# A decode attention kernel: the softmax bias moved from GpSimd to ScalarE, and the pipeline around it respaced

## Chip, cores and metric

The kernel runs on one core of a Trainium2 chip. The metric is device time in microseconds (us), the median over executions. A profile gives the span from the first to the last instruction, about 2 us less than the device time (819.8 against 821.6 us). A run counts as slow when it is over 1.5% above the fastest of the same kernel; fast runs are compared with fast runs.

Engines are named as in the profile: PE is TensorE (PEld is its loading of weights), DVE is VectorE, ACT is ScalarE, POOL is GpSimd, SP is the engine that issues the DMAs. "POOLq" or "SPq" is the sequencer of an engine.

## The reference

There are two grouped-query attention blocks for one new token, with separate inputs. Each has a batch of 4, 32 query heads, 8 key/value heads and a head size of 128. Problem A attends to all 4096 cached keys; problem B only to the last 1024.

```python
q = (x @ wq).reshape(B, 1, 32, 128)                  # x: 4 x 1 x 512, wq: 512 x 4096
scores = einsum("bhqd,bhkd->bhqk", q, k) * 128**-0.5 # k, v repeated 4x over heads
p = softmax(scores)
o = einsum("bhqk,bhkd->bhqd", p, v)
out = o.reshape(B, 1, 4096) @ wo                     # wo: 4096 x 512
# result: concatenate(A's out, B's out)
```

Almost all of the work is reading: the caches and weights are 100.7 MB in bf16, and each byte is used for a few products only.

## The kernel before

The work is cut into 40 units of 1 MB of K and 1 MB of V: 32 of problem A (one batch, one key/value head, 4096 keys) and then 8 of problem B (four batches, one head, 1024 keys each). For one unit:

1. SP loads K and V into SBUF, the working memory. PE transposes K in 32 blocks of 128x128 into PSUM, the memory for PE's results, in four groups of eight; DVE copies each group to SBUF.
2. PE computes the scores (32 matmuls of 4 columns). DVE reduces them to a maximum per partition. POOL makes the maximum over all partitions (a partition all-reduce), and multiplies it by minus the scale: that is the bias.
3. ACT computes the exponentials with that bias. DVE sums them per partition, and POOL sums over partitions with a second all-reduce (the denominator).
4. PE multiplies by V, DVE normalises, and for every group of heads PE adds the output projection.

POOL's loop and ACT's wait are what the argument is about:

```python
for t in range(self.NU):                       # 40 units
    self.wait(g_, f"dve.red.{t}")
    g_.partition_all_reduce(self.bm[:, s, 0:w], self.pm[:, s, 0:w], 128, ReduceOp.max)
    self.wait(g_, f"pool.max.{t}")
    ...
    g_.tensor_scalar(out=self.biasT[:, s, 0:w], in0=self.bm[:, s, 0:w],
                     scalar1=-self.scale, scalar2=None, op0=ALU.mult)
    if t - self.Ld >= 0:
        self._pool_den(g_, t - self.Ld)        # waits dve.rsum, partition_all_reduce(add)

# ACT, per unit
    self.wait(act, f"pool.bias.{i}")
    self.wait(act, f"pe.s.{i}")
    ...   # 4 exponentials of 128x32 (A) or 16 of 128x8 (B), bias=biasT column

# DVE, per step t
    self._dve_kcopies(dve, t + 2)
    self._dve_reduce(dve, t)
    self._dve_rowsum(dve, t - 1)
    self._dve_norm(dve, t - 1)                 # waits pool.den.{t-1}

# PE, per step t
    self._pe_transposes(pe, t + 1)             # two PSUM banks for the groups
    self._pe_scores(pe, t)
    self._pe_pv(pe, t - 2)
    # the output projection of unit t - 4; the whole second q projection after step 26
```

In DVE's program the copies for the next unit stand behind the wait for the denominator. In the trace DVE waits 20.53 us for POOL's denominator, starts the reciprocal at 306.20 us and the next copies at 306.49 us. A result that is late on POOL therefore holds up these copies, and through them PE and the freeing of load buffers.

## Time and profile before

| | before |
|---|---|
| device time, median of 5 | 824.1 us (819.7 to 825.1) |
| span of the profiled run | 819.8 us |
| busy: PE, DVE, ACT, POOL | 30%, 17%, 6%, 5% |
| mean DMA rate | 124 GB/s |
| mean granted PE clock | 0.527 |

The page of the kernel before: its busy line, and rows of 40 equal slices of the span (PEclk in tenths of full clock, DMA in tenths of busy, GB/s moved).

```profile
PE 244.2 (30%) x4168; PEld 210.3 (26%) x4168; DVE 136.4 (17%) x325; ACT 50.3 (6%) x257; POOL 44.7 (5%) x128
...
PEclk9855555555555555555555555565555555555555
DMA  8993222222223272222222333323833333110000
GB/s 355 388 405 135 103 102 103 104 103 103 103 103 103 103 307 103 103 103 103 103 103 103 107 106 124 118 86 109 277 103 108 124 123 109 52 52 1 1 1 1
```

No engine is busy, PE's granted clock is about half from the third slice on, and after three slices the loads fall from about 400 to about 103 GB/s. Nothing in this view is at a limit, so the kernel is held by waiting, not by work.

The waits, longest in total (engine, line, waited for: us in total, times, longest us):

```profile
ACT e_sb L350 <- POOL biasT L266: 733.9, 40, 23.6
DVE rden L639 <- POOL den L290: 621.1, 40, 21.3
...
POOL biasT L266 <- issue: 342.4, 40, 12.3
POOL den L290 <- issue: 244.3, 39, 10.9
```

ACT waits 734 of 820 us for the bias and DVE 621 us for the denominator; both come from POOL. POOL itself has 342 + 244 us before its own instructions in which it waits for nothing that the profile shows ("issue").

The timeline of POOL alone in steady state (start us, duration us, engine, line, operation, and in brackets the idle time before it and what ended it):

```profile
305.72 0.44 POOL L290 PARTITION_ALL_REDUCE den<-acc  x1 [10.88 <-issue]
310.14 0.38 POOL L254 PARTITION_ALL_REDUCE bm<-pm  x1 [3.98 <-DVE pm L608]
319.05 0.26 POOL L266 TENSOR_SCALAR biasT<-bm 128x4 f32<-128x4 f32 x1 [8.53 <-issue]
325.30 0.44 POOL L290 PARTITION_ALL_REDUCE den<-acc  x1 [5.99 <-issue]
```

One unit takes 19.6 us, from 305.72 to 325.30. The recorded work is 1.1 us. Between the all-reduce for the maximum and the multiply lie 8.5 us, and between the multiply and the next all-reduce 6.0 us. The wait of 3.98 us for DVE is the only one with a visible cause. The unit is typical, but for the 10.88 us before its first line: in the whole trace 36 of the 39 unexplained waits before the denominator's all-reduce are 5.8 to 6.3 us (the others 7.0, 8.8 and 10.9), and 38 of the 40 before the multiply are 6.9 to 9.2 us (the others 10.3 and 12.3).

Is an all-reduce itself slow, and its record only too short? At the end of the program two all-reduces follow each other. The timeline of all engines there:

```profile
812.77 0.44 POOL L290 PARTITION_ALL_REDUCE den<-acc  x1 [5.98 <-issue]
...
813.62 0.28 DVE L624 TENSOR_REDUCE acc<-e_sb 128x16 f32<-128x128 bf16 x1
...
814.00 0.44 POOL L290 PARTITION_ALL_REDUCE den<-acc  x1 [0.79 <-DVE acc L624]
...
814.48 0.25 DVE L639 RECIPROCAL rden<-den 128x16 f32<-128x16 f32 x1 [0.58 <-POOL den L290]
```

The second all-reduce starts 0.1 us after DVE's sum ends (813.62 + 0.28), and DVE goes on at 814.48. So an all-reduce after an all-reduce costs about half a microsecond; the 6 us are not its own.

### The profile page before, as it was taken

The numbers are of one execution on the slowest core, as the hardware profiler recorded it, in microseconds if no ns is written. First come the engines' busy times: TensorE is split into PE (matmuls) and PEld (weight loads), VectorE is DVE, ScalarE is ACT, GpSimd is POOL, SyncE is SP. The second block draws the span as 40 slices with busy tenths as digits, with TensorE's granted clock in tenths as the row PEclk, the third lists the DMA queues.
The fourth block names the chain that finished last, engine by engine and source line by source line (L and its number), as shares of the span: only waits on it lengthen the run. The fifth ranks groups of instructions, "written<-read, shape, count | busy, mean of one in ns | idle before, by whom it ended". The sixth has DMA issues, their size and how long they took to land.

```text
span 819.8 us, 9559 instructions
## 1 busy us (share of the span) xinstructions
PE 244.2 (30%) x4168; PEld 210.3 (26%) x4168; DVE 136.4 (17%) x325; ACT 50.3 (6%) x257; POOL 44.7 (5%) x128
## 2 busy tenths in 40 slices
PE   3512222322232303232323332332222322333323
PEld 3412222222222203232312232322222322222211
DVE  1401111111111101121111111121111111111100
ACT  0000000000000000000000000000000001111211
POOL 0000000000000000000000000000000000000000
PEclk9855555555555555555555555565555555555555
DMA  8993222222223272222222333323833333110000
GB/s 355 388 405 135 103 102 103 104 103 103 103 103 103 103 307 103 103 103 103 103 103 103 107 106 124 118 86 109 277 103 108 124 123 109 52 52 1 1 1 1
DMA packets 27019, 101.31 MB, mean 124 GB/s; under 512 B 1360, under 2 KB 9568, under 8 KB 17760
## 3 DMA queue, kind: packets, MB, share of 16 engines
q1 hardware_dynamic: 26976, 100.69, 33.4%
q8 instruction: 33, 0.54, 0.3%
q14 instruction: 10, 0.08, 0.0%
HBM read 100.67 MB, written 0.01 MB: 123 GB/s over the span
## 4 chain that ended last, share of the span: by engine, by line
issue 89%; POOL 5%; PE 2%; DMA 2%; DVE 1%; POOLq 1%; ACT 0%; SPq 0%
POOL den L290 2%; POOL bm L254 2%; DMA big_w<-in_A_wq_dram 2%; PE KTps L442 1%; POOL biasT L266 1%; DVE KT L592 1%; PE outp L512 0%; PE psT L416 0%; POOLq L266 0%; POOLq L290 0%; PE psT L471 0%; ACT e_sb L350 0%; DVE out_sb L572 0%; DVE rden L639 0%; DVE pm L608 0%
## 5 line engine op out<-in xcount | busy, mean ns | idle before, releaser
L442 PE MATMUL KTps<-ident,rawKd 128*128 128x128 bf16 x896 | 101.6, 304 | 334.2 <-DVE KT L592 334.2
L442 PEld LDWEIGHTS KTps<-ident,rawKd 128*128 128x128 bf16 x896 | 87.3, 141 | 349.0 <-DVE KT L592 341.4
L592 DVE COPY KT<-KTps 128x1024 bf16<-128x1024 bf16 x160 | 106.5, 687 | 28.5 <-PE KTps L442 28.0
L639 DVE RECIPROCAL rden<-den 128x4 f32<-128x4 f32 (+1 forms) x40 | 7.7, 193 | 621.1 <-POOL den L290 621.1
L442 PE MATMUL KTps<-ident,big_w 128*128 128x128 bf16 x384 | 44.2, 307 | 181.2 <-DVE KT L592 168.3
L350 ACT ACTIVATE e_sb<-psT,biasT 128x32 bf16<-128x32 f32 (+1 forms) x256 | 49.0, 330 | 733.9 <-POOL biasT L266 733.9
L442 PEld LDWEIGHTS KTps<-ident,big_w 128*128 128x128 bf16 x384 | 38.1, 143 | 185.7 <-DVE KT L592 171.3
L491 PE MATMUL oT<-e_sb,V 128*128 128x4 bf16 x1280 | 39.7, 166 | 42.5 <-ACT e_sb L350 42.5
L491 PEld LDWEIGHTS oT<-e_sb,V 128*128 128x128 bf16 x1280 | 37.2, 104 | 44.5 <-issue 44.5
L471 PEld LDWEIGHTS psT<-qT_sb,KT 128*128 128x128 bf16 x1280 | 41.6, 106 | 0.9 <-issue 0.9
L471 PE MATMUL psT<-qT_sb,KT 128*128 128x4 bf16 x1280 | 41.1, 167 | 0.0
L290 POOL PARTITION_ALL_REDUCE den<-acc x40 | 17.7, 443 | 245.1 <-issue 244.3
L266 POOL TENSOR_SCALAR biasT<-bm 128x4 f32<-128x4 f32 (+1 forms) x40 | 10.6, 264 | 342.4 <-issue 342.4
L254 POOL PARTITION_ALL_REDUCE bm<-pm x40 | 15.5, 387 | 172.5 <-DVE pm L608 165.8
L512 PE MATMUL outp<-big_w,OT_all 128*4 128x512 bf16 x32 | 14.8, 621 | 1.4 <-DVE OT_all L646 1.4
L512 PE MATMUL outp<-wo_sb,OT_all 128*4 128x512 bf16 x32 | 14.1, 590 | 0.0
L624 DVE TENSOR_REDUCE acc<-e_sb 128x4 f32<-128x128 bf16 (+1 forms) x40 | 11.1, 277 | 10.8 <-ACT e_sb L350 10.8
L608 DVE TENSOR_REDUCE pm<-psT 128x4 f32<-128x128 f32 (+1 forms) x40 | 11.2, 281 | 0.0
L646 DVE TENSOR_TENSOR OT_all<-oT,rden 128x4 bf16<-128x4 f32 (+1 forms) x40 | 6.9, 173 | 1.4
L512 PEld LDWEIGHTS outp<-big_w,OT_all 128*4 128x4 bf16 x32 | 2.9, 107 | 7.8 <-issue 5.1
L416 PE MATMUL psT<-xT_sb,big_w 128*128 128x4 bf16 x128 | 3.6, 166 | 3.5 <-DMA big_w<-in_A_wq_dram 3.5
L416 PEld LDWEIGHTS psT<-xT_sb,big_w 128*128 128x128 bf16 x128 | 3.5, 104 | 3.6 <-DMA big_w<-in_A_wq_dram 3.6
(18 smaller groups left out, 15.7 us busy)
## 6 DMA issues: line engine op xcount, KB each, us to landing
V<-in_A_v_cache_dram SPq DMA_DIRECT2D x32, 1024.0 KB, 5.1
rawKd<-in_A_k_cache_dram SPq DMA_DIRECT2D x22, 1024.0 KB, 7.4
big_w<-in_A_k_cache_dram SPq DMA_DIRECT2D x10, 1024.0 KB, 7.3
V<-in_B_v_cache_dram SPq DMA_DIRECT2D x8, 1024.0 KB, 5.6
rawKd<-in_B_k_cache_dram SPq DMA_DIRECT2D x6, 1024.0 KB, 8.2
big_w<-in_A_wq_dram SPq DMA_DIRECT2D x1, 4096.0 KB, 12.6
wo_sb<-in_A_wo_dram SPq DMA_DIRECT2D x1, 4096.0 KB, 29.0
big_w<-in_B_wq_dram SPq DMA_DIRECT2D x1, 4096.0 KB, 14.8
```

Of the source, the lines that this page charges most:

```text
L254: g_.partition_all_reduce(self.bm[:, s, 0:w], self.pm[:, s, 0:w], 128, bass.bass_isa.ReduceOp.max)
L266: g_.tensor_scalar(out=self.biasT[:, s, 0:w], in0=self.bm[:, s, 0:w], scalar1=-self.scale, scalar2=None, op0=ALU.mult,)
L290: g_.partition_all_reduce(self.den[:, s, 0:w], self.acc[:, s, 0:w], 128, bass.bass_isa.ReduceOp.add)
L350: ins = act.activation(self.e_sb[:, se, b * C:(b + 1) * C, h], ps[:, b * C:(b + 1) * C, h], ACT_F.Exp, bias=self.biasT[:, sy, idx:idx + 1] ...
L442: ins = pe.transpose(self.KTps[kb][:, k, :], self.Rq(r)[:, q0 + k, :], self.ident128[:, :],)
L471: ins = pe.matmul(ps[:, q, :], lhsT=KTv[:, q, :], rhs=qT, start=True, stop=True)
L491: ins = pe.matmul(self.oT[ob][:, b * 4:(b + 1) * 4], lhsT=self.Vq(s)[:, q, :], rhs=self.e_sb[:, se, q, :], start=(c == 0), stop=(c == C - 1),)
L512: ins = pe.matmul(self.outp[0:self.NB, :], lhsT=self.OT_all[P][:, h, :], rhs=self.wo_sb[P][:, h, :], start=(h == 0), stop=(h == self.HQ - 1),)
L592: ins = dve.tensor_copy(dst[:, q0:q0 + ng, :], self.KTps[kb][:, 0:ng, :])
L608: ins = dve.reduce_max(self.pm[:, sy, 0:w], ps, axis=AX.X)
L624: ins = dve.reduce_sum(self.acc[:, sy, 0:w], ev, axis=AX.X)
L639: ins = dve.reciprocal(self.rden[:, sy, 0:w], self.den[:, sy, 0:w])
```

## The change

The intent was to take the multiply off POOL and then let the rest of the pipeline run closer. The diff has about 300 lines; this is its core.

```diff
 # POOL: only all-reduces are left in the loop
             self.inc(ins, "pool", f"pool.max.{t}")
-            self.wait(g_, f"pool.max.{t}")
-            if t - NY >= 0:
-                self.wait(g_, f"act.exp.{t - NY}.last")
-            ins = g_.tensor_scalar(out=self.biasT[:, s, 0:w], in0=self.bm[:, s, 0:w],
-                                   scalar1=-self.scale, scalar2=None, op0=ALU.mult)
-            self.inc(ins, "pool", f"pool.bias.{t}")
 # ACT: the bias is a copy with a scale
-        self.wait(act, f"pool.bias.{i}")
+        self.wait(act, f"pool.max.{i}")
+        ins = act.activation(self.biasT[:, sy, 0:w], self.bm[:, sy, 0:w], ACT_F.Copy,
+                             scale=-self.scale)
+        self.inc(ins, "act", f"act.bias.{i}")
+        self.wait(act, f"act.bias.{i}")
 # configuration: lead of the copies, banks for transposes, lead of the K loads
-    LK=2,
+    LK=1,
+    NKTB=4,
-    KLEAD=2,
+    KLEAD=3,
 # PE: values before scores, second q projection in eight chunks instead of at once
             if t + LT < self.NU:
                 self._pe_transposes(pe, t + LT)
+            if 0 <= i < self.NU:
+                k = step - self.QB0
+                if 0 <= k < self.NPIECE:
+                    self._pe_qTB_chunk(pe, i, k)
+                self._pe_pv(pe, i)
             if t < self.NU:
                 self._pe_scores(pe, t)
-            if 0 <= i < self.NU:
-                self._pe_pv(pe, i)
...
 # SP: four K and four V blocks asked for in advance, weights in pieces
+        for t in range(NRD):
+            self._issue_k(sp, t)
+        for t in range(NRD):
+            self._issue_v(sp, t)
...
+            for P, key in ((0, "wo0_at"), (1, "wo1_at")):
+                p = t - self.cfg[key]
+                if 0 <= p < self.NPIECE:
+                    self._issue_wo(sp, P, p)
```

To get the two further PSUM banks for transposes, the result of the value product moved into a free part of the score bank. A switch for filler matmuls and one for loads that transpose are in the diff but turned off.

## The prediction

> **What bounds the kernel now.** The page's busy table shows no full engine: PE 30%, DVE 17%, ACT 6%, POOL 5%, and DMA moves 101.3 MB at a mean of 124 GB/s. The chain of waits is 89% "issue", through POOL's three lines. In the time-ordered listing one unit of steady state (POOL operations at 305.72, 310.14, 319.05, 325.30 us) is 19.6 us: an all-reduce for the maximum (0.38 us), 8.5 us in which POOL shows nothing, the small multiply for the bias (0.26 us), 6.0 us of nothing, the all-reduce for the denominator (0.44 us), then 4.0 us in which POOL waits for DVE. 40 units of 19.6 us are 784 of the 820 us. The waits agree: ACT waits 734 us for the bias, DVE 621 us for the denominator.

> The two gaps are not the all-reduce itself. Where one all-reduce follows another, there is no gap: at the end (812.77, then 814.00 us) the second starts 0.1 us after DVE's sum ends, and DVE goes on 0.6 us after that sum. So a gap comes with each change between the all-reduce and the ordinary multiply. [...]the trace has 5.9 to 6.2 us into the all-reduce, and 7 to 8.8 us the other way.

> **What the change does.** The multiply goes to ACT as a copy with a scale; POOL then runs only all-reduces in the loop. That removes about 14.5 us from every unit's chain and adds some 0.3 us on ACT. [...]I expect still one table load (1.28 us now). The rest (four transpose banks, loads issued earlier and in pieces, second projection in eight chunks) serves a pipeline that isn't POOL-bound.

> **The new bound.** Estimates per unit of problem A from the trace's durations: DVE four copies 2.7, two reductions and the wait for POOL about 1.3, normalising 0.3: 4.3 us. PE 4.2 us at full clock (transposes 66 ns, as at 24 to 31 us) but 6.3 us at half clock (118 ns). POOL about 1 us. DMA: 2.1 MB; with a full queue the windows between 8 and 32 us show 412 to 427 GB/s, so 5.05 us. So DMA bounds next: 92 MB at 415 GB/s is 222 us, the two output weights (8.4 MB in 1 KB rows, 349 GB/s in the window where the first arrives) 25 us; 2 us of start, about 8 us after the last byte, 2 us from span to device time, some 7 us of stalls: 266 us. If PE stayed at half clock, it would bound instead: about 295 us.

> **Prediction.** 266 us, 8 in 10 between 254 and 296. Faster by over 2%: 0.985; within 2%: 0.01; slower: 0.005.

> **What would show it.** Right: the 6 and 8.5 us gaps on POOL gone, units spaced 5.0 to 5.6 us, DMA busy nine tenths in nearly all slices at about 400 GB/s, ACT with one table load, PE clock well over 0.5. Wrong: gaps of 6 us before all-reduces that follow all-reduces; table loads at every unit; DMA below 350 GB/s.

> **What could make it wrong.** PE at half clock; DVE, which waits in order on POOL, on the second projection's chunks and on the scores, taking over 5.05 us a unit; issue blocked by buffer waits; the gaps having another cause than alternation.

Its sum: 222 + 25 + 2 + 8 + 2 + 7 = 266 us. The 0.3 us on ACT (an exponential takes 0.33 us in the kernel before), the 8 us after the last byte and the 7 us of stalls are estimates; the text doesn't say from which numbers.

## More of the kernel before

The chain that ended last, in order of time, has one more hint (start us, us, what):

```profile
310.14 0.38 POOL bm L254
310.52 0.07 POOLq L266 x2
310.59 8.46 issue
```

Right after the all-reduce, POOL's sequencer handles two instructions of line 266, the line of the multiply, which is one instruction in the source; then 8.46 us show nothing.

## The result

| | before | after |
|---|---|---|
| device time, median | 821.9 us (15 runs) | 268.16 us (8 runs, 267.4 to 269.6) |
| ratio of fast runs | | 0.3263 (95%: 0.3254 to 0.3273) |
| span | 819.8 us | 266.2 us |
| busy: PE, DVE, ACT, POOL | 30, 17, 6, 5% | 80, 49, 22, 12% |
| mean DMA rate over the span | 124 GB/s | 380 GB/s |
| mean granted PE clock | 0.527 | 0.717 |

Ratios here are the mean time of one kernel's fast runs over that of the other's in the same rounds, so not quite the ratio of the medians. The kernel is 3.06 times as fast; 266 us had been predicted.

The page of the kernel after, the same rows:

```profile
PE 212.6 (80%) x4168; PEld 190.1 (71%) x4168; DVE 129.9 (49%) x332; ACT 58.5 (22%) x297; POOL 32.7 (12%) x88
...
PEclk9999757555775867557555777997956767589955
DMA  6999999999999999999999999999999999999820
GB/s 214 430 421 419 414 419 403 403 401 402 402 406 397 401 413 423 415 419 416 417 416 417 413 403 396 402 399 403 401 396 390 407 396 380 384 386 386 325 84 1
```

The loads are busy nine tenths or more from the second slice to the 37th, at about 400 GB/s. Now a resource is at its limit for most of the span.

POOL's timeline in steady state:

```profile
152.46 0.37 POOL L293 PARTITION_ALL_REDUCE bm<-pm  x1 [3.38 <-DVE pm L682]
152.74 0.51 POOL L316 PARTITION_ALL_REDUCE den<-acc  x1
157.91 0.37 POOL L293 PARTITION_ALL_REDUCE bm<-pm  x1 [4.66 <-DVE pm L682]
158.18 0.51 POOL L316 PARTITION_ALL_REDUCE den<-acc  x1
```

Here the two all-reduces (the maximum of a unit and the denominator of the unit before it) follow each other with no idle time in between, and the maximum's waits only for DVE. Both gaps are gone: in the whole trace every wait of these all-reduces is for DVE. Around the eight chunks of the second projection the denominator's all-reduce waits, too, 1.6 to 4.2 us for DVE's sum.

The waits of the kernel after:

```profile
ACT biasT L376 <- POOL bm L293: 198.4, 39, 22.8
POOL bm L293 <- DVE pm L682: 192.9, 40, 12.9
DVE OT_all L735 <- PE psT L565: 59.9, 37, 8.7
DVE rden L728 <- POOL den L316: 27.3, 40, 0.8
```

DVE's wait for the denominator fell from 621 to 27 us, which is 0.7 us a unit. ACT and POOL still wait, now for other engines; whether the loads or the engines set the pace is tested in experiment 9.

The page's summary of the chain that ended last, by engine:

```profile
PE 44%; DMA 39%; SPq 8%; DVE 6%; issue 2%; DVEq 0%
```

The chain before was 89% "issue". Now it goes through loads and PE.

How the stages differ is seen in windows of the span (start and end: length, busy us and count of PE, PE weight loads, DVE, ACT, POOL, then PE clock, DMA share, GB/s):

```profile
100.00:120.00 20.00, 18.39 (x341) 16.55 (x339) 9.89 (x27) 2.67 (x13) 2.41 (x6) 0.59 1.01 418
...
160.00:180.00 20.00, 18.12 (x422) 16.55 (x419) 14.06 (x36) 4.30 (x20) 3.13 (x8) 0.91 1.03 401
...
220.00:240.00 20.00, 18.08 (x330) 15.63 (x328) 10.62 (x27) 8.93 (x53) 3.24 (x8) 0.70 1.04 382
...
250.00:256.00 6.00, 5.21 (x108) 3.16 (x104) 3.70 (x10) 3.93 (x27) 1.20 (x3) 0.69 0.58 212
256.00:262.00 6.00, 6.00 (x75) 2.80 (x74) 1.47 (x6) 3.11 (x20) 0.88 (x2) 0.50 0.00 0
```

Between 80 and 180 us, where problem A is loaded, such windows show 401 to 418 GB/s. The loads of problem B, whose rows are 2 KB instead of 8 KB, run at 382. In the last 6 us of loading only 58% of the DMA engines' time is busy, and from about 256 us to the end of the span at 266 us nothing is loaded.

### The profile page after: what moved, and what is told of

Same layout as the page of the kernel before. It is cut to its first block, busy times and chain, and to the rows that moved or that the text cites. A ratio compares the mean times of both kernels' runs of the same rounds, so it can differ in the third digit from the quotient of the medians.

```text
span 266.2 us, 9426 instructions
## 1 busy us (share of the span) xinstructions
PE 212.6 (80%) x4168; PEld 190.1 (71%) x4168; DVE 129.9 (49%) x332; ACT 58.5 (22%) x297; POOL 32.7 (12%) x88
## 4 chain that ended last, share of the span: by engine, by line
PE 44%; DMA 39%; SPq 8%; DVE 6%; issue 2%; DVEq 0%
PE KTps L504 24%; DMA rawKd<-in_A_k_cache_dram 22%; PE psT L565 8%; DMA big_w<-in_A_k_cache_dram 7%; PE outp L586 7%; DMA big_w<-in_B_k_cache_dram 6%; DMA big_w<-in_A_wq_dram 5%; SPq L236 4%; PE psT L545 3%; DVE KT L666 3%; SPq L211 2%; PE psT L452 1%; PE psT L477 1%; SPq L248 1%; SPq L194 1%
## 5 line engine op out<-in xcount | busy, mean ns | idle before, releaser
L666 DVE COPY KT<-KTps 128x1024 bf16<-128x1024 bf16 x160 | 99.1, 681 | 0.5 <-PE KTps L504 0.5
L504 PE MATMUL KTps<-ident,rawKd 128*128 128x128 bf16 x896 | 80.5, 270 | 14.8 <-DMA rawKd<-in_A_k_cache_dram 9.2
L504 PEld LDWEIGHTS KTps<-ident,rawKd 128*128 128x128 bf16 x896 | 74.2, 125 | 21.9 <-DMA rawKd<-in_A_k_cache_dram 11.0
L376 ACT ACTIVATE biasT<-bm 128x4 f32<-128x4 f32 (+1 forms) x40 | 8.4, 210 | 198.4 <-POOL bm L293 198.4
L504 PE MATMUL KTps<-ident,big_w 128*128 128x128 bf16 x384 | 36.1, 275 | 13.3 <-DMA big_w<-in_A_k_cache_dram 10.9
L565 PEld LDWEIGHTS psT<-e_sb,V 128*128 128x128 bf16 x1280 | 38.2, 100 | 10.1 <-issue 7.9
L565 PE MATMUL psT<-e_sb,V 128*128 128x4 bf16 x1280 | 39.6, 166 | 5.9 <-DVE acc L698 3.3
L504 PEld LDWEIGHTS KTps<-ident,big_w 128*128 128x128 bf16 x384 | 32.6, 127 | 16.3 <-DMA big_w<-in_A_k_cache_dram 11.5
L545 PEld LDWEIGHTS psT<-qT_sb,KT 128*128 128x128 bf16 x1280 | 36.2, 99 | 2.8 <-issue 2.8
L735 DVE TENSOR_TENSOR OT_all<-psT,rden 128x4 bf16<-128x4 f32 (+1 forms) x40 | 6.9, 174 | 60.2 <-PE psT L565 59.9
L316 POOL PARTITION_ALL_REDUCE den<-acc x40 | 19.6, 491 | 23.9 <-DVE acc L698 23.9
## 6 DMA issues: line engine op xcount, KB each, us to landing
rawKd<-in_B_k_cache_dram SPq DMA_DIRECT2D x6, 1024.0 KB, 14.5
big_w<-in_A_wq_dram SPq DMA_DIRECT2D x1, 4096.0 KB, 12.6
```

The source lines that it names most:

```text
L316: g_.partition_all_reduce(self.den[:, s, 0:w], self.acc[:, s, 0:w], 128, bass.bass_isa.ReduceOp.add)
L376: ins = act.activation(self.biasT[:, sy, 0:w], self.bm[:, sy, 0:w], ACT_F.Copy, scale=-self.scale)
L504: ins = pe.transpose(self.KTps[kb][:, k, :], self.Rq(r)[:, q0 + k, :], self.ident128[:, :],)
L545: ins = pe.matmul(ps[:, q, :], lhsT=KTv[:, q, :], rhs=qT, start=True, stop=True)
L565: ins = pe.matmul(self.oT[ob][:, b * 4:(b + 1) * 4], lhsT=self.Vq(s)[:, q, :], rhs=self.e_sb[:, se, q, :], start=(c == 0), stop=(c == C - 1),)
L666: ins = dve.tensor_copy(dst[:, q0:q0 + ng, :], self.KTps[kb][:, 0:ng, :])
```

## Experiments

The theory after the prediction had two parts. First, POOL's switching between the all-reduce and the multiply made the old time. Second, the loads bound the new kernel. Rivals were that the respaced pipeline brought a good part of the gain; that the gaps came from waiting on POOL's own result or from any operation on POOL; and that engines waiting on each other, not the loads, set the new pace.

### 1. The bias moved, and nothing else

The kernel before, with only the POOL and ACT parts of the diff above; the load order, the two banks and PE's order are the old ones.

> The kernel before with one edit alone: the bias is made on ACT (copy with a scale) and POOL runs only all-reduces in the loop; the order of PE, the two transpose banks and the old load order stay. Theory (the alternation on POOL is nearly all of the gain): the 6 and 8.5 us gaps are gone and the time is 270 to 320 us, most likely 285; what is left over 268 us is what the other edits are worth. Rival (the rest of the change is needed to get most of the gain): over 350 us.

Measured: correct, 270.9 and 271.0 us in the two fast runs; two more runs at 275.2 and 275.3 count as slow (their granted clocks, 0.78 and 0.77, are close to the 0.80 and 0.78 of the fast ones, and none of the eight runs of the kernel after was slow; why is open). The kernel before took 816.7 us on the same chip. In the same rounds two variants of the kernel after that differ from it by idle memsets (experiments 3 and 4) took 268.2 and 268.5 us. So the one moved operation brings 546 of 548 us, over 99%. All the other edits together are worth about 2.5 us in fast runs. POOL's timeline shows both gaps gone here too:

```profile
156.69 0.37 POOL L254 PARTITION_ALL_REDUCE bm<-pm  x1 [5.12 <-DVE pm L603]
156.96 0.50 POOL L277 PARTITION_ALL_REDUCE den<-acc  x1
```

### 2. The bias put back on POOL in the kernel after

```diff
+            self.wait(g_, f"pool.max.{t}")
+            ...
+            ins = g_.tensor_scalar(out=self.biasT[:, s, 0:w], in0=self.bm[:, s, 0:w], ...)
...
-        ins = act.activation(self.biasT[:, sy, 0:w], self.bm[:, sy, 0:w], ACT_F.Copy, ...)
+        self.wait(act, f"pool.bias.{i}")
```

> The kernel after with one edit undone: the multiply for the bias is back on POOL between the two all-reduces. Theory: gaps of about 6 us before the denominator's all-reduce and 7 to 9 us before the multiply come back in every unit, units are spaced 18 to 20 us, the time is 740 to 820 us. Rival (the restructured pipeline hides the gaps): under 600 us.

Measured: 746.5 us, correct, ratio to before 0.9147. Gaps of 7.0 and 6.0 us were back and units were 17.2 us apart. The whole respaced pipeline without the moved bias takes 8.5% off the time; the moved bias without it takes off two thirds.

### 3 and 4. An idle memset, and four of them

```diff
             self.inc(ins, "pool", f"pool.max.{t}")
+            for r in range(1):     # or 4
+                ins = g_.memset(self.junk[:, 4 * t + r:4 * t + r + 1], 0.0)
+                self.inc(ins, "pool", f"pool.junk.{t}.{r}")
```

> The kernel after with one small memset of an unused tile on POOL in every unit, between the two all-reduces; no engine waits for it and it waits for nothing. Theory (each change between the all-reduce and an ordinary operation costs, whatever the operation's data): both gaps come back, about 14 us a unit, the denominator is late by as much, and the time is 700 to 820 us. Rival (the gaps come from POOL waiting on its own semaphore for the all-reduce's result, or from the multiply itself): under 300 us.

> As the run with one memset, but with four memsets one after the other at the same place in every unit. Theory (the change of kind costs, not the operation): within 20 us of the run with one memset. Rival (every ordinary operation of POOL is slow to start, some 8 us each): 24 us more a unit, over 1600 us.

Measured: 268.5 us with one memset, 268.2 us with four. This expectation failed: it isn't true that any change of operation costs. POOL's timeline in the run with one memset:

```profile
151.13 0.37 POOL L293 PARTITION_ALL_REDUCE bm<-pm  x1 [3.38 <-DVE pm L687]
151.38 0.17 POOL L303 MEMSET junk<- 128x1 f32 x1
151.44 0.51 POOL L321 PARTITION_ALL_REDUCE den<-acc  x1
```

The memset runs between the two all-reduces with no idle time on either side. The order of instructions in the built program explains what is different. This is the listing of POOL's instructions for a unit of the kernel before and for the memset variant; "ISA" with operands is an all-reduce, and "ISA" alone is an instruction that the source doesn't have:

```
kernel before                        with one memset
L254 ISA bm<-pm 128x4                L293 ISA bm<-pm 128x4
L266 ISA                             L303 Memset junk 128x1
L266 TensorScalarPtr biasT<-bm       L321 ISA den<-acc 128x4
L290 ISA
L290 ISA den<-acc 128x4
```

### 5. An idle multiply

```diff
             self.inc(ins, "pool", f"pool.max.{t}")
+            ins = g_.tensor_scalar(out=self.junk[:, 4 * t:4 * t + 4], in0=self.zero4[:, :],
+                                   scalar1=-self.scale, scalar2=None, op0=ALU.mult)
+            self.inc(ins, "pool", f"pool.junk.{t}")
```

> The kernel after with one small multiply on POOL between the two all-reduces of every unit: its input is a constant tile, its output is never read, no engine waits for it and it waits for nothing. The memset at this place cost nothing, so the theory is narrower now: it isn't any change of operation that costs, but the change between the all-reduce and an operation for which the built program puts an extra operand-less instruction in front of it and in front of the next all-reduce (the listing of the built program shows that for the multiply, not for the memset). Theory: both gaps (about 7 and 6 us) come back and the time is 720 to 770 us, like the run with the bias back on POOL (746.5). Rival (the gaps come from POOL waiting for its own all-reduce's result, and ACT and DVE waiting for the multiply): under 300 us, like the memset.

Measured: 743.1 us, correct. The timeline of POOL:

```profile
160.34 0.38 POOL L297 PARTITION_ALL_REDUCE bm<-pm  x1 [3.10 <-DVE pm L697]
167.75 0.26 POOL L307 TENSOR_SCALAR junk<-zero 128x4 f32<-128x4 f32 x1 [7.03 <-issue]
173.91 0.44 POOL L331 PARTITION_ALL_REDUCE den<-acc  x1 [5.90 <-issue]
```

Nobody uses this multiply and it waits for nothing, and still 7.0 and 5.9 us stand before it and after it. That takes away the rivals of data dependence and of the wait on POOL's own semaphore: the time is within 4 us of that with the real bias on POOL.

### 6. The idle multiply in every fourth unit

The edit is that of experiment 5 under `if t % 4 == 3`.

> The same idle multiply, but only in every fourth unit: 10 pairs of gaps of 13.1 us. Theory: compute stops for about 13 us ten times, and between the stops a unit takes 4.1 to 4.4 us where data is ready; the loads run on meanwhile while buffers are free. 10 x (4 x 4.3 + 13.1) plus about 30 us at both ends gives 335 us; 310 to 360 us. Rival (loads run so far ahead that the stops are hidden): under 290 us.

Measured: 393.1 us, above the expected 310 to 360 us. The sign and the rival's fall are clear, but the size was wrong, in two terms that the trace gives. The ten pairs of gaps took 92.5 + 64.4 us, so 15.7 us a pair instead of 13.1. The eight multiplies that waited while loads ran at 329 to 411 GB/s waited 7.5 to 11.3 us, the two at 218 and 2 GB/s 6.9 us; so full-rate loading goes with longer gaps here, but no run varies it alone. That is 26 us. The other 32 us are in the units between: (392 - 157 - 30) / 40 is 5.1 us instead of 4.3. In eight stretches between the stops PE is busy 89% of the time, at clocks of 0.58 to 0.89, and two of the stretches have chunks of the second projection (see experiment 8); how much each of these costs was not separated.

### 7. An idle affine select

```diff
+            ins = g_.affine_select(out=self.junk[:, 4 * t:4 * t + 4], in_=self.zero4[:, :],
+                                   compare_op=ALU.not_equal, fill=1.0, ...)
```

> The same place, with an affine select of a constant tile instead of the multiply in every unit. It computes on data as the multiply does, but the listing of the built program shows no extra instruction before it or before the all-reduce after it. Theory: no gap, 266 to 272 us. Rival (every operation with arithmetic on POOL costs, only a memset is free): 720 us or more.

Measured: 267.7 us, correct. The timeline of POOL:

```profile
154.49 0.37 POOL L297 PARTITION_ALL_REDUCE bm<-pm  x1 [3.56 <-DVE pm L698]
154.75 0.25 POOL L307 TENSOR_SCALAR_AFFINE_SELECT junk<-zero 128x4 f32<-128x4 f32 x1
154.91 0.50 POOL L332 PARTITION_ALL_REDUCE den<-acc  x1
```

This operation computes on data as the multiply does, takes about as long (0.25 us), and costs nothing. Together with 3 to 5 that separates the causes: of the three operations tried between the all-reduces, only the multiply costs, and the listing of the built program told which, before the run. At the start of the program an affine select does stand after a gap: in the kernel after, one of the two pairs of sequencer records belongs to it, and POOL waits 9.80 us before it with no visible cause. So it is not the kind of operation alone that makes the gap.

### 8 and 9. Fewer bytes, and less work

Experiment 8 loads half of each V block and uses it twice. Experiment 9 makes and copies half of the transposes and uses them twice. Both compute something else.

```diff
 # 8
-                        lhsT=self.Vq(s)[:, q, :],
+                        lhsT=self.Vq(s)[:, q % 16, :],     # and loads of [:, :, 0:C // 2, :]
 # 9
-            for q0 in range(0, self.Q, 8):
+            for q0 in range(0, self.Q // 2, 8):            # and KTv[:, q % 16, :]
```

> The kernel after, loading only half of each V block and using it twice: 21 of 100.7 MB less, all engines' work unchanged (wrong result on purpose). Theory (the loads bound the kernel after): 215 to 240 us, where compute at 4.1 to 4.4 us a unit starts to bound. Rival (the engines waiting on each other set the 5.2 us a unit): over 258 us.

> The kernel after with half of the transposes and half of the copies out of their banks, each used twice; all loads unchanged (wrong result on purpose). That takes 1 to 1.9 us a unit from PE and 1.2 us from DVE. Theory (loads bound): 260 to 268 us, only the end gets a little shorter. Rival (engines bound): under 240 us.

Measured in 9: 266.7 us, within 0.6% of the kernel after, although PE's busy time fell from 212.6 to 179.1 us and DVE's from 129.9 to 82.6 us. (The output passed the comparison even so.) The page's chain for that run:

```profile
DMA 76%; PE 12%; SPq 10%; issue 1%; DVE 0%
```

With less work on the engines the chain goes to the loads and the time stays; the two runs had mean clocks of 0.716 and 0.588 and took 266.3 and 267.1 us. So the loads bound the kernel after. The chain of the kernel after alone did not say so: it gave PE 44% and DMA 39%.

Measured in 8: wrong result, 248.6 us in the only fast run (254.7 us in the profiled one, which counts as slow). That lies between the two expectations. 21% fewer bytes gave 7%, so a second limit stands close behind the loads, and my estimate of 4.1 to 4.4 us a unit for it was too good. Windows of the loads, first of experiment 8 (its slow run, read for its structure only), then of the kernel after:

```profile
120.00:130.00 10.00, 9.07 (x155) 8.87 (x153) 4.73 (x14) 2.14 (x10) 1.17 (x3) 0.50 0.83 304
130.00:140.00 10.00, 9.32 (x180) 7.76 (x181) 4.42 (x14) 1.07 (x5) 1.23 (x3) 0.61 0.26 87
```

```profile
120.00:130.00 10.00, 8.96 (x194) 8.57 (x192) 3.90 (x13) 1.62 (x9) 1.24 (x3) 0.67 1.02 418
130.00:140.00 10.00, 9.27 (x166) 9.10 (x163) 5.99 (x15) 1.45 (x7) 1.18 (x3) 0.50 1.01 414
```

In experiment 8 the loads almost stop (87 GB/s) at 130 to 140 us, because the buffers are full: in these steps PE and DVE exchange the eight chunks of the second projection, and a unit takes 6.7 us (from the starts of the maximum's all-reduce, 95.22 to 141.94 us in 7 units). In the kernel after the same steps take 6.8 us a unit (98.41 to 152.46 us in 8), while 2.1 MB at 415 GB/s take 5.05 us. It runs at 414 to 418 GB/s all the same, from requests that were queued before; 8 units later the deficit is about 14 us, and it is paid off afterwards, where units take down to 4.1 us. In these four windows PE is busy 9.0 to 9.3 of 10 us at a clock of 0.50 to 0.67, and DVE 3.9 to 6.0 us; so PE below its full clock is nearest to being the second limit there. The risk that the prediction named is real, but it is absorbed.

### 10 and 11. The end of the program

The last byte lands at about 256 us and the span ends at 266 us. Experiment 10 reorders the last three units; experiment 11 adds filler matmuls, to test whether PE's clock then stays up.

```diff
 # 10, DVE, last three units: reduce first, then copy; PE: last scores before the value product
+            if late and t < self.NU - 1:
+                self._dve_reduce(dve, t)
             if t + LK < self.NU:
                 self._dve_kcopies(dve, t + LK)
 # 11, in addition, before each of the last three value products
+            for f in range(16):
+                pe.matmul(self.KTps_t[0][0:4, 0:128], lhsT=self.qT_sb[1][:, 0, 0:4],
+                          rhs=self.ident128[:, :], start=True, stop=True)
```

> The kernel after with another order in the last three units alone: DVE reduces the scores before it copies the next unit's transposes, and PE computes the last scores before it waits for the third last V block. The last byte lands about 256 us into the span, the end comes 10 us later through two sets of 16 exponentials. Theory: the exponentials of the last two units come 2 us earlier, 1 to 4 us gained, 264 to 267 us. Rival (the last V block or PE at half clock sets the end): no gain, 268 us. It is meant to be correct.

> As the run with the other order at the end, plus 16 matmuls whose result is not used before each of the last three value products[...]. In the kernel after the clock falls to half at 252 us and the last 20 matmuls of the output projection take 0.44 us each instead of 0.24. Theory: 2 to 4 us less than without the filler, 261 to 265 us. Rival: the filler delays the end as much as the clock gains, no difference. It is meant to be correct.

Measured: 269.1 us (268.7 to 270.1) and, in the fast runs, 270.0 to 272.9 us. Both are misses. In 10 the reductions came earlier, but they delayed the copies: the last scores waited 2.3 us for them and started at 255.06 us, against 253.79 us in the kernel after. In 11 the clock didn't rise in the last microseconds. The windows there, of the kernel after and of 11 (a profiled run that counts as slow, read for its structure only):

```profile
256.00:262.00 6.00, 6.00 (x75) 2.80 (x74) 1.47 (x6) 3.11 (x20) 0.88 (x2) 0.50 0.00 0
```

```profile
256.00:262.00 6.00, 6.00 (x80) 4.55 (x78) 1.07 (x5) 3.21 (x20) 0.89 (x3) 0.50 0.00 0
```

In both, PE is busy for all of these 6 us and keeps a clock of 0.50; in 11 it stays at 0.50 until 270 us. In the kernel after it was 0.50 from 254 us to the end of PE's work at about 264 us, with PE busy without a pause. So a busy PE alone did not bring it up here. In 11 the first filler starts only at 256.34 us, when the clock has already fallen (0.64 in the window from 254 to 256 us). So the filler, 1.9 us for each set of 16, took time and didn't raise the clock again; what an earlier one would have done was not tested.

### 12. Problem B first

A version that was to beat both kernels: the 8 units of B come first, so the program ends on a unit with 4 exponentials instead of 16 and with one output projection group outstanding.

```diff
-        for g in range(self.HKV):
-            for b in range(self.NB):
-                self.units.append((0, g, b, 1))
+        for g in range(self.HKV):
+            self.units.append((0, g, 0, self.NB))
         self.NUA = len(self.units)
+        for g in range(self.HKV):
+            for b in range(self.NB):
+                self.units.append((1, g, b, 1))
 # inputs, offsets and the halves of the output swapped accordingly;
 # second projection in four chunks of eight heads in steps 4 to 7; weights asked for earlier
```

> The kernel after with the two problems in the other order: the 8 units of problem B first, then the 32 of problem A; the projection of A in four chunks in steps 4 to 7, the weights asked for earlier. Bytes and work per unit stay. Meant to be correct. The end of the kernel after is 10 us of work after the last byte: two sets of 16 exponentials of 0.166 us and 12 matmuls of the output projection at half clock. With A last it is 4 exponentials of 0.22 us a unit and 4 such matmuls, and B's loads in 2 KB rows come where compute isn't ready anyway. Theory (loads bound, plus the end): 3 to 6 us less, 262 to 265 us against 268.2. Rival (the end is set by when the last V block lands, or the early weights starve the start): 267 us or more.

Measured: correct, 264.67 us (264.3 to 265.7, five fast runs), ratio to before 0.3249 (0.3237 to 0.3261). The end of its timeline, all engines:

```profile
257.29 0.94 PEld L566 LDWEIGHTS psT<-e_sb,V 128*128 128x128 bf16 x32 [0.54 <-DMA V<-in_A_v_cache_dram]
...
260.54 0.68 DVE L649 CAST out_sb<-outp 4x512 bf16<-4x512 f32 x1 [1.96 <-PE outp L587]
```

The weight load of the last value product waits for the load of its V block until 257.29 us (the last exponentials end at 257.2 us, too), and the last copy of the output starts 3.3 us later; the span is 262.9 us. All five runs are below all eight of the kernel after (267.4 to 269.6), but they are not from the same rounds: before took 815.5 us there and 821.9 us beside the kernel after. Variants of the kernel after with harmless POOL operations took 267.7 to 268.5 us on chips where before took 816.7 and 818.3 us, so the chip explains little of it. By the medians the gain is 1.3%; by the ratios to the kernel before (0.3249 and 0.3263) it is 0.4%, with intervals that overlap. Either is under the 2% that count as faster, and the size of the gain is open. The edit also changes the chunks and when weights are loaded, so the order alone was not tested.

## Why the prediction was right

- **The cause.** It named the switch between the all-reduce and the multiply, from the gaps of one unit and from the one place with two all-reduces in a row. Experiments 1, 2 and 5 confirm this pair. The wider reading of experiment 3, that any ordinary operation does the same, was wrong: a memset and an affine select are free (3, 4, 7).
- **What is removed.** About 14.5 us a unit off POOL's chain, said the prediction. Both gaps are gone in every unit of the trace. The time fell by 13.8 us a unit (554 / 40) and not more, because the loads took over as the limit.
- **What is added.** About 0.3 us on ACT was estimated; the copy takes 0.21 us on average (8.4 us in 40). The whole trace has one table load (1.28 us), as expected, although 40 copies alternate with the exponentials.
- **The new bound.** Loads, said the prediction, and experiment 9 shows it. The sum of its terms up to the last byte, 2 + 222 + 25 + 7 = 256 us, is what the windows show: the DMA engines are busy 70%, 56% and 47% in the three 2-us windows before 256 us, and idle after. Single terms were off and cancelled: problem B runs at 382 to 386 GB/s, below the 415 assumed, and the output weights in pieces don't pull the rate down to the 349 assumed (401 to 410 GB/s in 140 to 180 us, where the second of them is loaded). That the sum came so close is in part luck.
- **The end.** 8 us were given to it after the last byte; it took 10, at half clock. With that, the total of 266 us was 2 us short of 268.2.
- **PE's clock.** Expected well over 0.5: 0.717, but not full. PE had 4.2 us a unit at full clock by estimate; in windows at a clock of 0.59 it was busy 18 of 20 us. The second limit is therefore closer than I had written, as experiment 8 shows.
- **The spacing.** 5.0 to 5.6 us a unit was announced as a sign. The mean is 5.92 us ((255.21 - 24.33) / 39), because 12.6 MB of later weights share the stream of loads (by estimate 0.8 us a unit at 415 GB/s); this sign was stated wrongly, though the sum had the weights.

What stays open: that the build adds an instruction for the multiply in the loop and none for the affine select is read off the built program, not explained; the half clock of the last 10 us has no settled cause; and the rate of problem B's loads (382 to 386 GB/s with 2 KB rows, beside about 415 with 8 KB rows) was not tested by varying the row size alone.

## What to carry to other kernels

When no engine is busy, look for gaps that repeat before the same small instruction, compare them with a place where the neighbour is different, and list the built program there: an instruction that the source doesn't have, in front of both neighbours, was here the mark of a price paid at every alternation (8.5 and 6.0 us in the unit shown), and moving one cheap operation to another engine removed it. After such a move expect the next limit to set the gain: it was the loads here (by experiment 9, not by the chain's shares), and they left only some 2.5 us to all the rest of a large change. Test which limit it is by taking away bytes and work separately, for the second limit may stand only a few per cent behind.
